# Sigmoid attention and two feed-forward layers on one core: first loads from two queues, values later, and products of zeros at the start

## Chip, cores and metric

The kernel runs on one core of a Trainium2 chip. The metric is the device time of one execution in microseconds (us). Three runs of the kernel before took 1111.2, 1111.86 and 1110.76 us; their median is 1111.2 us. A profiled execution is one more run, with its own time.

## What is computed

The inputs are float32 queries, keys and values of shape (4, 12, 448, 64), that is batch, heads, sequence and head size. The attention has a sigmoid in place of a softmax; two feed-forward layers over 1792 tokens follow. The reference, cut to what matters:

```python
scores = scale * np.matmul(q, k.transpose(0, 1, 3, 2)) - np.log(S)
attn = 1.0 / (1.0 + np.exp(-scores))
x = np.matmul(attn, v)                 # then (batch, S, heads * 64): 1792 x 768
h = x @ moe_w_in;  x = np.maximum(h, 0.0) ** 2 @ moe_w_out       # 768 -> 2048 -> 768
h = x @ moe2_w_in
out = (np.maximum(h, 0.0) + alpha * np.minimum(h, 0.0)) @ moe2_w_out
```

## The kernel before, in words

A unit is one batch entry and one pair of heads: 4 x 6 = 24 units, two heads of 64 rows side by side on the 128 partitions. Of the 448 positions of the sequence, 384 are three blocks of 128 (`MAIN`, `R = 3`) and 64 are a remainder (`REM`). Two units share their remainders, so the attention runs in 12 turns `d` of a loop over units `u = 2d` and `w = 2d + 1`. The order of all instructions is written out by hand: every engine takes its instructions in the order of the program (`tc.manual_schedule`), and each waits only for the data and buffers that it needs.

`fetch(d)` (lines 127 to 144) issues all loads of two units on SyncE's queue. Per unit these are two loads of queries, one for each head, into the tile `nat` (line 142), one of the queries' remainder into `qk` (line 144), three of the keys in the same way, one of the values (`v`, line 139) and one of their remainder (`vrem`, line 144): eight issues a unit, sixteen a turn. The tag `nat` has two buffers, so the next two units' queries can be issued only when the transposes of the last two are done.

`turn(u)` (lines 150 to 159) transposes queries and keys on TensorE (PE), seven transposes into a PSUM tile of the tag `big`, and VectorE copies the result to `flat`. `part(u)` and `rest(u)` (lines 161 to 167) split `flat` on VectorE into a rounded part and the difference. `scores(u, j)` (lines 169 to 178) makes the scores of one block of 128 keys with six products (three pairs; the second and third need the difference), and ScalarE takes the sigmoid out of PSUM. `last_scores(d)` (lines 180 to 188) does the same for the remainders of both units out of `flat`, eight products. The tag `big` has three buffers, shared in turn by transposes and scores. `values(u)` (lines 190 to 196) multiplies with the values, twelve products a unit, `last_values(d)` (lines 198 to 204) with the remainders, and `finish(u)` (lines 206 to 215) writes the result, split in two parts, into the x tiles on ScalarE and VectorE.

The start (lines 217 to 223) is `fetch(0)`, the load of alpha, `turn`, `part` and `rest` for units 0 and 1, then `fetch(1)`. A turn `d` of the loop (lines 224 to 257) has on PE, in this order: remainder scores of `d`, remainder values of `d - 1`, three score groups of `u`, values of `w - 2`, the transposes of units `u + 2` and `w + 2`, three score groups of `w`, values of `u`. In the first turn nothing of an earlier turn is there. SyncE's `fetch(d + 2)` stands behind the two transposes. Loads of the feed-forward weights (lines 66 to 72) and their assembly out of 64-bit floats are spread over later turns and the feed-forward layers. These (lines 268 to 361) run blocks of two 128-wide slices of the hidden layer over four tiles of tokens; their products are lines 276 and 309.

The program's first instructions are an identity matrix on GpSimd, a memset of the sigmoid's bias on VectorE, and a first sigmoid on one column, which brings ScalarE's function table (lines 113 to 116).

Of the kernel before, what the change touches and what calls it, by code (L numbers as in the profile page):

```python
# [9 lines left out]
F32 = mybir.dt.float32  # L10
# [5 lines left out]
P = 128  # L16
# [3 lines left out]
def fused_kernel(ctx: ExitStack, tc: tile.TileContext, q, k, v, w1i, w1o, w2i, w2o, alpha, out):  # L20
# [31 lines left out]
    wpool = ctx.enter_context(tc.tile_pool(name="wpool", bufs=1))  # L52

    eye = const.tile([P, P], F32, name="eye")
    bias = const.tile([P, 1], F32, name="bias")
    al = const.tile([P, NF], F32, name="al")


# [51 lines left out]
        return x[layer, t, c]  # L110

    with tc.manual_schedule():
        make_identity(nc, eye)
        nc.vector.memset(bias, -math.log(S))

        nc.scalar.activation(al[:, :1], bias, AF.Sigmoid)


        with tc.tile_pool(name="apool", bufs=1) as apool, tc.tile_pool(name="apsum", bufs=1, space=bass.MemoryType.PSUM) as psum:
            units = [(b, c) for b in range(B) for c in range(H // 2)]  # L120
            ND = len(units) // 2
            nats, qks, vals, vrems, flats, parts, sig, avs = {}, {}, {}, {}, {}, {}, {}, {}

            def half(u):
                return slice(u % 2 * REM, (u % 2 + 1) * REM)

            def fetch(d):
                if d >= ND:
                    return
                vrems[d] = apool.tile([P, 2, D], F32, tag="vrem", name=f"vrem{d}", bufs=3)  # L130
                for u in (2 * d, 2 * d + 1):
                    b, c = units[u]
                    hs = slice(2 * c, 2 * c + 2)
                    nats[u] = apool.tile([P, 2, R, 2, D], F32, tag="nat", name=f"nat{u}", bufs=2)
                    vals[u] = apool.tile([P, 2, R, D], F32, tag="v", name=f"v{u}", bufs=5)
                    qks[u] = apool.tile([P, 2, D], F32, tag="qk", name=f"qk{u}", bufs=2)
                    for j, src in enumerate((q, k, v)):
                        if j == 2:
                            nc.sync.dma_start(out=vals[u], in_=src[b, hs, :MAIN, :].rearrange("h (p r) d -> p h r d", r=R))
                        else:  # L140
                            for h in range(2):
                                nc.sync.dma_start(out=nats[u][:, j, :, h, :], in_=src[b, 2 * c + h, :MAIN, :].rearrange("(p r) d -> p r d", r=R))  # L142
                        last = (qks[u][:REM], qks[u][REM:], vrems[d][half(u)])[j]
                        nc.sync.dma_start(out=last, in_=src[b, hs, MAIN:, :].rearrange("h p d -> p h d"))

            def big(name):

                return psum.tile([P, 1024], F32, tag="big", name=name, bufs=3)

            def turn(u):  # L150

                ps = big(f"tp{u}")
                for r in range(R):
                    nc.tensor.transpose(ps[:, r * P:(r + 1) * P], nats[u][:, 0, r].rearrange("p h d -> p (h d)"), eye)  # L154
                nc.tensor.transpose(ps[:, MAIN:MAIN + P], qks.pop(u).rearrange("p h d -> p (h d)"), eye)
                for r in range(R):
                    nc.tensor.transpose(ps[:, 512 + r * P:512 + (r + 1) * P], nats[u][:, 1, r].rearrange("p h d -> p (h d)"), eye)  # L157
                flats[u] = apool.tile([P, 2 * S], F32, tag="flat", name=f"flat{u}", bufs=2)
                nc.vector.tensor_copy(flats[u], ps[:, :2 * S])

            def part(u):

                parts[u] = [apool.tile([P, 2 * S], F32R, tag=f"qk{p}", name=f"qk{p}{u}", bufs=3) for p in "hl"]
                nc.vector.tensor_copy(parts[u][0], flats[u])

            def rest(u):
                nc.vector.tensor_sub(parts[u][1], flats[u], parts[u][0])

            def scores(u, j):
                hi, lo = parts[u]  # L170
                ps = big(f"sc{u}_{j}").rearrange("p (h s) -> p h s", h=2)
                at = 512 + j * P
                for i, (kt, qt) in enumerate(((hi, hi), (hi, lo), (lo, hi))):
                    for h in range(2):
                        rows = slice(h * D, (h + 1) * D)
                        nc.tensor.matmul(ps[:, h, :S], kt[rows, at:at + P], qt[rows, :S], start=(i == 0), stop=(i == 2))  # L176
                sig[u, j] = apool.tile([P, 2, S], F32, tag="a", name=f"a{u}_{j}", bufs=5)
                nc.scalar.activation(sig[u, j], ps[:, :, :S], AF.Sigmoid, bias=bias, scale=SCALE)

            def last_scores(d):  # L180

                ps = big(f"scr{d}").rearrange("p (h s) -> p h s", h=2)
                for h in range(2):
                    rows = slice(h * D, (h + 1) * D)
                    for u in (2 * d, 2 * d + 1):
                        nc.tensor.matmul(ps[half(u), h, :S], flats[u][rows, S:S + REM], flats[u][rows, :S], start=True, stop=True)  # L186
                sig[d] = apool.tile([P, 2, S], F32, tag="ar", name=f"ar{d}", bufs=2)
                nc.scalar.activation(sig[d], ps[:, :, :S], AF.Sigmoid, bias=bias, scale=SCALE)

            def values(u):  # L190
                for j in range(R):
                    a = sig.pop((u, j))
                    if u % 2 == 0 and j == 0:
                        avs[u] = psum.tile([P, 512], F32, tag="av", name=f"av{u}", bufs=2)
                    for h in range(2):
                        nc.tensor.matmul(avs[u][h * D:(h + 1) * D, :S], vals[u][:, h, j, :], a[:, h, :], start=(u % 2 == 0 and j == 0), stop=(u % 2 == 1 and j == R - 1))  # L196

            def last_values(d):

                a, w, u = sig.pop(d), vrems.pop(d), 2 * d  # L200
                avs[u + 1] = psum.tile([P, 512], F32, tag="av", name=f"av{u + 1}", bufs=2)
                for h in range(2):
                    for i in (u, u + 1):
                        nc.tensor.matmul(avs[i][h * D:(h + 1) * D, :S], w[half(i), h, :], a[half(i), h, :], start=(i > u), stop=(i == u))  # L204

            def finish(u):
                b, c = units[u]
                ps = avs.pop(u)
                for t, (first, n) in enumerate(TILES):
                    lo, hi = max(first, b * S), min(first + n, (b + 1) * S)  # L210
                    if lo < hi:
                        xh, xl = (p[:, lo - first:hi - first] for p in x_tiles(0, t, c))
                        out_ = ps[:, lo - b * S:hi - b * S]
                        nc.scalar.activation(xh, out_, AF.Copy)
                        nc.vector.tensor_sub(xl, out_, xh)

            fetch(0)
            nc.sync.dma_start(out=al, in_=alpha.rearrange("(f p) -> p f", p=P))
            for u in (0, 1):
                turn(u)  # L220
                part(u)
                rest(u)
            fetch(1)
            for d in range(ND):
                u, w = 2 * d, 2 * d + 1

                i = d - 4
                last_scores(d)
                if d:
                    last_values(d - 1)  # L230
                    finish(u - 2)
                if 0 < i < 7:
                    assemble(i - 1, 1)
                for j in range(R):
                    scores(u, j)
                if d:
                    values(w - 2)
                if d + 1 < ND:
                    turn(u + 2)
                    turn(w + 2)  # L240
                    fetch(d + 2)
                if d:
                    finish(w - 2)
                if d + 1 < ND:
                    part(u + 2)
                    rest(u + 2)
                    part(w + 2)
                    rest(w + 2)
                if d in (1, 2, 3):
                    load(d - 1)  # L250
                if 0 <= i < 6:
                    assemble(i, 0)
                if 0 < i < 7:
                    split(i - 1)
                for j in range(R):
                    scores(w, j)
                values(u)
            last_values(ND - 1)
            finish(2 * ND - 2)
            values(2 * ND - 1)  # L260
            finish(2 * ND - 1)
# [130 lines left out]
```

## Time and profile before

| what | value |
|---|---|
| median of three runs | 1111.2 us (1110.76 to 1111.86) |
| the profiled execution's own time | 1112.57 us |
| its span, first to last instruction | 1110.8 us |
| mean granted clock of PE | 0.996 |
| busy: PE, VectorE, ScalarE, GpSimd | 1087.2, 691.8, 347.7, 154.5 us |

The span is one profiled execution. PE is the matrix engine, PEld its weight loads, DVE VectorE, ACT ScalarE, POOL GpSimd, SP SyncE, and SPq SyncE's queue of DMA issues. A row of the timeline gives start and length in us, engine, line, instruction, output and inputs with shapes, count, and in brackets how long the engine had been idle and what released it. Products are pipelined, so the length of one is more than the distance to the next. The granted clock (PEclk) is 1.00 at 2.4 GHz. A DMA share is the mean busy share of the core's 16 DMA engines.

### The profile page before, as it was taken

The numbers are of one execution on the slowest core, as the hardware profiler recorded it, in microseconds if no ns is written. First come the engines' busy times: TensorE is split into PE (matmuls) and PEld (weight loads), VectorE is DVE, ScalarE is ACT, GpSimd is POOL, SyncE is SP. The second block draws the span as 40 slices with busy tenths as digits, with TensorE's granted clock in tenths as the row PEclk, the third lists the DMA queues.
The fourth block names the chain that finished last, engine by engine and source line by source line (L and its number), as shares of the span: only waits on it lengthen the run. The fifth ranks groups of instructions, "written<-read, shape, count | busy, mean of one in ns | idle before, by whom it ended". The sixth has DMA issues, their size and how long they took to land.

```text
span 1110.8 us, 14450 instructions
## 1 busy us (share of the span) xinstructions
PE 1087.2 (98%) x5880; PEld 942.4 (85%) x5880; DVE 691.8 (62%) x991; ACT 347.7 (31%) x524; POOL 154.5 (14%) x94
## 2 busy tenths in 40 slices
PE   5999999999999999999999999999999999999998
PEld 3555557989898998989898999999999898989898
DVE  3458872345656575756666664577676767677554
ACT  2667773442222231323224444211121212021110
POOL 0001110020202020201014641101020201020000
PEclk9999999999999999999999999999999999999999
DMA  5575650020202121111111111202020202110015
GB/s 111 125 175 139 170 137 1 29 86 24 81 11 86 29 86 29 61 54 57 58 58 57 57 58 43 72 30 86 29 86 26 72 18 86 29 58 30 1 57 142
DMA packets 89266, 73.30 MB, mean 66 GB/s; under 512 B 52592, under 2 KB 83312, under 8 KB 89200
## 3 DMA queue, kind: packets, MB, share of 16 engines
q1 hardware_dynamic: 89200, 72.38, 22.8%
q8 instruction: 46, 0.75, 0.3%
q14 instruction: 20, 0.16, 0.0%
HBM read 66.85 MB, written 5.51 MB: 65 GB/s over the span
## 4 chain that ended last, share of the span: by engine, by line
PE 92%; DVE 4%; ACT 2%; SPq 1%; DMA 0%; issue 0%; ACTq 0%
PE h L276 40%; PE o L309 39%; PE av L196 5%; PE sc L176 5%; DVE raw L87 1%; SPq L142 1%; PE scr L186 1%; PE av L204 1%; DVE r L286 1%; PE tp L154 1%; DVE g L287 1%; PE tp L157 1%; ACT gh L288 1%; DVE raw L88 1%; ACT raw L83 1%; ACT wh L98 1%
## 5 line engine op out<-in xcount | busy, mean ns | idle before, releaser
L276 PE MATMUL h<-xh,wl 128*128 128x512 f32 (+1 forms) x768 | 278.5, 363 | 0.0
L276 PE MATMUL h<-xl,wh 128*128 128x512 f32 (+1 forms) x768 | 278.3, 362 | 0.0
L276 PE MATMUL h<-xh,wh 128*128 128x512 f32 (+1 forms) x768 | 277.9, 362 | 0.0
L314 DVE TENSOR_TENSOR acc<-o,acc 128x384 f32<-128x384 f32 (+1 forms) x364 | 200.1, 584 | 76.9 <-PE o L309 75.4
L99 POOL TENSOR_TENSOR wl<-raw,wh 128x768 fp32r<-128x768 f32 x64 | 124.2, 1941 | 883.8 <-ACT wh L98 835.8
L276 PEld LDWEIGHTS h<-xh,wh 128*128 128x128 f32 x768 | 144.2, 188 | 15.6 <-issue 0.7
L309 PE MATMUL o<-wh,gh 128*128 128x384 f32 x448 | 150.6, 336 | 6.5 <-DVE acc L314 6.2
L276 PEld LDWEIGHTS h<-xh,wl 128*128 128x128 f32 x768 | 144.1, 188 | 15.1
L276 PEld LDWEIGHTS h<-xl,wh 128*128 128x128 f32 x768 | 144.1, 188 | 15.0
L309 PE MATMUL o<-wl,gh 128*128 128x384 f32 x448 | 149.9, 335 | 0.0
L309 PE MATMUL o<-wh,gl 128*128 128x384 f32 x448 | 149.8, 334 | 0.0
L309 PE MATMUL o<-gh,wl 128*128 128x512 f32 (+1 forms) x384 | 139.1, 362 | 0.0
L309 PE MATMUL o<-gl,wh 128*128 128x512 f32 (+1 forms) x384 | 139.0, 362 | 0.0
L309 PE MATMUL o<-gh,wh 128*128 128x512 f32 (+1 forms) x384 | 138.9, 362 | 0.0
L288 ACT ACTIVATE gh<-g 128x512 fp32r<-128x512 f32 (+1 forms) x64 | 37.0, 579 | 284.6 <-DVE g L287 284.6
L289 DVE TENSOR_TENSOR gl<-g,gh 128x512 fp32r<-128x512 f32 (+1 forms) x128 | 93.5, 730 | 52.3 <-ACT gh L288 45.4
L98 ACT ACTIVATE wh<-raw 128x768 fp32r<-128x768 f32 x64 | 57.4, 897 | 175.3 <-DVE raw L88 129.4
L283 DVE SCALAR_TENSOR_TENSOR g<-h,r 128x512 f32<-128x512 f32 (+1 forms) x64 | 39.9, 623 | 113.4 <-ACT r L282 113.4
L87 DVE SCALAR_TENSOR_TENSOR raw<-raw 128x768 int32<-128x768 int32 x64 | 81.1, 1267 | 30.1 <-ACT raw L83 25.7
L282 ACT ACTIVATE r<-h 128x512 f32<-128x512 f32 (+1 forms) x64 | 34.8, 543 | 186.0 <-PE h L276 185.5
L309 PEld LDWEIGHTS o<-wh,gh 128*128 128x128 f32 x448 | 84.1, 188 | 9.4 <-DVE acc L314 8.1
L286 DVE TENSOR_SCALAR r<-h,al 128x512 f32<-128x512 f32 (+1 forms) x64 | 43.6, 681 | 71.4 <-PE h L276 71.3
(47 smaller groups left out, 1191.3 us busy)
## 6 DMA issues: line engine op xcount, KB each, us to landing
raw<-in_moe_w_in_dram SPq DMA_DIRECT2D x32, 768.0 KB, 4.9
raw<-in_moe_w_out_dram SPq DMA_DIRECT2D x32, 768.0 KB, 4.4
nat<-in_q_dram SPq DMA_DIRECT2D x48, 96.0 KB, 2.9
nat<-in_k_dram SPq DMA_DIRECT2D x48, 96.0 KB, 2.9
v<-in_v_dram SPq DMA_DIRECT2D x24, 192.0 KB, 2.9
out_dram<-acc SPq DMA_DIRECT2D x16, 192.0 KB, 2.7
out_dram<-acc SPq DMA_DIRECT2D x6, 384.0 KB, 2.3
qk<-in_q_dram SPq DMA_DIRECT2D x24, 32.0 KB, 2.6
```

Source lines behind the costliest of these rows:

```text
L87: nc.vector.scalar_tensor_tensor(out=low, in0=high, scalar=3, in1=low, op0=ALU.logical_shift_left, op1=ALU.bitwise_or)
L98: nc.scalar.activation(hi, w, AF.Copy)
L99: nc.gpsimd.tensor_sub(lo, w, hi)
L176: nc.tensor.matmul(ps[:, h, :S], kt[rows, at:at + P], qt[rows, :S], start=(i == 0), stop=(i == 2))
L196: nc.tensor.matmul(avs[u][h * D:(h + 1) * D, :S], vals[u][:, h, j, :], a[:, h, :], start=(u % 2 == 0 and j == 0), stop=(u % 2 == 1 and j = ...
L276: nc.tensor.matmul(ps[:, :n], wp[:, c * P:(c + 1) * P], xp, start=(c == 0 and i == 0), stop=(c == NC - 1 and i == 2))
L283: nc.vector.scalar_tensor_tensor(out=gt, in0=ps[:, :n], scalar=0.0, in1=r, op0=ALU.max, op1=ALU.mult)
L286: nc.vector.tensor_scalar(out=r, in0=ps[:, :n], scalar1=0.0, scalar2=al[:, f:f + 1], op0=ALU.min, op1=ALU.mult)
L288: nc.scalar.activation(gh, gt, AF.Copy)
L289: nc.vector.tensor_sub(gl, gt, gh)
L309: nc.tensor.matmul(ps[:, :size], *ops, start=(i == 0), stop=(i == len(turns) - 1))
L314: nc.vector.tensor_add(part, ps[:, :size], part)
```

## The change

The queries and keys of the first two turns (units 0 to 3) are issued at once at the start, queries on SyncE's queue and keys on ScalarE's. Units 2 and 3 get buffers of their own for this, borrowed from the weights' tag `woh`. Values are issued by a function of their own, `fetch_values`: behind the queries at the start, and later one turn ahead, behind the loads of queries and keys. The first sigmoid stands behind ScalarE's DMA issues and no longer writes into alpha's tile. `qk` has four buffers instead of two, `vrem` two instead of three. A tile of zeros is made first (in the storage of an x tile), and `keep_busy(n)` makes n products of zeros, 128 x 128 with 448 columns, which nothing reads: 10 before the first unit's transposes, 4 before the second unit's, 4 before the loop, and 6 in the first turn behind the remainder scores. The start's order is also changed: unit 1's transposes and their copy come before unit 0's difference.

```diff
--- before.py
+++ after.py
@@ -52,7 +52,7 @@
     wpool = ctx.enter_context(tc.tile_pool(name="wpool", bufs=1))
 
     eye = const.tile([P, P], F32, name="eye")
-    bias = const.tile([P, 1], F32, name="bias")
+    bias = const.tile([P, 2], F32, name="bias")
     al = const.tile([P, NF], F32, name="al")
 
 
@@ -110,10 +110,10 @@
         return x[layer, t, c]
 
     with tc.manual_schedule():
+        zeros = x_tiles(0, 0, 0)[0][:, :S]
+        nc.vector.memset(zeros.bitcast(F32), 0.0)
+        nc.vector.memset(bias, -math.log(S))
         make_identity(nc, eye)
-        nc.vector.memset(bias, -math.log(S))
-
-        nc.scalar.activation(al[:, :1], bias, AF.Sigmoid)
 
 
         with tc.tile_pool(name="apool", bufs=1) as apool, tc.tile_pool(name="apsum", bufs=1, space=bass.MemoryType.PSUM) as psum:
@@ -124,24 +124,32 @@
             def half(u):
                 return slice(u % 2 * REM, (u % 2 + 1) * REM)
 
-            def fetch(d):
+            def fetch(d, other=nc.sync):
+
                 if d >= ND:
                     return
-                vrems[d] = apool.tile([P, 2, D], F32, tag="vrem", name=f"vrem{d}", bufs=3)
                 for u in (2 * d, 2 * d + 1):
                     b, c = units[u]
                     hs = slice(2 * c, 2 * c + 2)
-                    nats[u] = apool.tile([P, 2, R, 2, D], F32, tag="nat", name=f"nat{u}", bufs=2)
+
+                    pool, tag, n = (wpool, "woh", 3) if d == 1 else (apool, "nat", 2)
+                    nats[u] = pool.tile([P, 2, R, 2, D], F32, tag=tag, name=f"nat{u}", bufs=n)
+                    qks[u] = apool.tile([P, 2, D], F32, tag="qk", name=f"qk{u}", bufs=4)
+                    for j, (src, queue) in enumerate(((q, nc.sync), (k, other))):
+                        for h in range(2):
+                            queue.dma_start(out=nats[u][:, j, :, h, :], in_=src[b, 2 * c + h, :MAIN, :].rearrange("(p r) d -> p r d", r=R))
+                        queue.dma_start(out=qks[u][j * REM:(j + 1) * REM], in_=src[b, hs, MAIN:, :].rearrange("h p d -> p h d"))
+
+            def fetch_values(d):
+                if d >= ND:
+                    return
+                vrems[d] = apool.tile([P, 2, D], F32, tag="vrem", name=f"vrem{d}", bufs=2)
+                for u in (2 * d, 2 * d + 1):
+                    b, c = units[u]
+                    hs = slice(2 * c, 2 * c + 2)
                     vals[u] = apool.tile([P, 2, R, D], F32, tag="v", name=f"v{u}", bufs=5)
-                    qks[u] = apool.tile([P, 2, D], F32, tag="qk", name=f"qk{u}", bufs=2)
-                    for j, src in enumerate((q, k, v)):
-                        if j == 2:
-                            nc.sync.dma_start(out=vals[u], in_=src[b, hs, :MAIN, :].rearrange("h (p r) d -> p h r d", r=R))
-                        else:
-                            for h in range(2):
-                                nc.sync.dma_start(out=nats[u][:, j, :, h, :], in_=src[b, 2 * c + h, :MAIN, :].rearrange("(p r) d -> p r d", r=R))
-                        last = (qks[u][:REM], qks[u][REM:], vrems[d][half(u)])[j]
-                        nc.sync.dma_start(out=last, in_=src[b, hs, MAIN:, :].rearrange("h p d -> p h d"))
+                    nc.sync.dma_start(out=vals[u], in_=v[b, hs, :MAIN, :].rearrange("h (p r) d -> p h r d", r=R))
+                    nc.sync.dma_start(out=vrems[d][half(u)], in_=v[b, hs, MAIN:, :].rearrange("h p d -> p h d"))
 
             def big(name):
 
...
-                nc.scalar.activation(sig[u, j], ps[:, :, :S], AF.Sigmoid, bias=bias, scale=SCALE)
+                nc.scalar.activation(sig[u, j], ps[:, :, :S], AF.Sigmoid, bias=bias[:, :1], scale=SCALE)
 
             def last_scores(d):
 
...
@@ -214,13 +222,28 @@
                         nc.scalar.activation(xh, out_, AF.Copy)
                         nc.vector.tensor_sub(xl, out_, xh)
 
-            fetch(0)
+            def keep_busy(n):
+
+                ps = psum.tile([P, 512], F32, tag="av", name=f"busy{n}", bufs=2)
+                for _ in range(n):
+                    nc.tensor.matmul(ps[:, :S], zeros[:, :P], zeros, start=True, stop=True)
+
+            fetch(0, nc.scalar)
+            fetch(1, nc.scalar)
+            fetch_values(0)
             nc.sync.dma_start(out=al, in_=alpha.rearrange("(f p) -> p f", p=P))
-            for u in (0, 1):
-                turn(u)
-                part(u)
-                rest(u)
-            fetch(1)
+
+            nc.scalar.activation(bias[:, 1:], bias[:, :1], AF.Sigmoid)
+            keep_busy(10)
+            turn(0)
+            part(0)
+            keep_busy(4)
+            turn(1)
+            rest(0)
+            part(1)
+            rest(1)
+            keep_busy(4)
+            fetch_values(1)
             for d in range(ND):
                 u, w = 2 * d, 2 * d + 1
 
@@ -229,6 +252,8 @@
                 if d:
                     last_values(d - 1)
                     finish(u - 2)
+                else:
+                    keep_busy(6)
                 if 0 < i < 7:
                     assemble(i - 1, 1)
                 for j in range(R):
@@ -239,6 +264,8 @@
                     turn(u + 2)
                     turn(w + 2)
                     fetch(d + 2)
+                    if d:
+                        fetch_values(d + 1)
                 if d:
                     finish(w - 2)
                 if d + 1 < ND:
```

## Rows read from the trace of the kernel before

**Rows 1.** The page's part 4: the chain that ended last, by engine

```profile
PE 92%; DVE 4%; ACT 2%; SPq 1%; DMA 0%; issue 0%; ACTq 0%
```

**Rows 2.** Waits of PE: engine line waited for: us in total, times, longest

```profile
PE tp L154 <- DMA nat<-in_q_dram: 8.0, 3, 4.6
PE o L309 <- DVE acc L314: 6.2, 6, 1.0
PE tp L155 <- DMA qk<-in_k_dram: 4.3, 3, 1.8
```

**Rows 3.** Windows: length, busy time of PE, PEld, DVE, ACT, POOL, PEclk, DMA share, GB/s

```profile
4.00:6.00 2.00, 0.87 (x3) 0.50 (x3) 0.00 (x0) 0.00 (x0) 0.00 (x0) 1.00 0.52 118
22.00:24.00 2.00, 0.52 (x3) 0.31 (x3) 0.00 (x0) 0.00 (x0) 0.00 (x0) 0.78 0.56 122
28.00:30.00 2.00, 2.00 (x12) 0.91 (x10) 1.94 (x3) 1.01 (x1) 0.00 (x0) 0.51 0.64 155
...
54.00:55.00 1.00, 1.00 (x10) 0.46 (x8) 0.97 (x3) 1.00 (x2) 0.00 (x0) 1.00 1.15 355
```

**Rows 4.** Timeline, PE, start and loop's second turn: start, length, line, tiles [idle before]

```profile
6.72 0.45 PE L155 MATMUL tp<-eye,qk 128*128 128x128 f32 x1 [1.28 <-DMA qk<-in_k_dram]
...
12.77 3.02 PE L186 MATMUL scr<-flat 64*64 64x448 f32 x8
...
19.37 0.70 PE L154 MATMUL tp<-eye,nat 128*128 128x128 f32 x3
...
24.43 0.45 PE L155 MATMUL tp<-eye,qk 128*128 128x128 f32 x1 [1.82 <-DMA qk<-in_k_dram]
...
31.91 0.98 PE L186 MATMUL scr<-flat 64*64 64x448 f32 x8
...
44.38 0.98 PE L186 MATMUL scr<-flat 64*64 64x448 f32 x8
```

**Rows 5.** Chain of waits in order of time, score products: start, length

```profile
25.52 3.66 PE sc L176 x18
...
33.65 2.02 PE sc L176 x18
```

**Rows 6.** Timeline, SyncE's DMA issues: start, length, line, tile

```profile
0.73 1.35 SPq L142 DMA_DIRECT2D nat<-in_q_dram  x2
...
4.12 0.62 SPq L144 DMA_DIRECT2D qk<-in_k_dram  x1
...
21.93 0.62 SPq L144 DMA_DIRECT2D qk<-in_k_dram  x1
...
39.02 1.23 SPq L142 DMA_DIRECT2D nat<-in_q_dram  x2
```

**Rows 7.** The page's part 6, one row: issues, KB each, us to landing

```profile
nat<-in_q_dram SPq DMA_DIRECT2D x48, 96.0 KB, 2.9
```

**Rows 8.** DMA view of 56.87 to 69.36 us, the same load

```profile
nat<-in_q_dram SPq DMA_DIRECT2D x4, 96.0 KB, 4.1
```

**Rows 9.** Timeline, VectorE and ScalarE at the start

```profile
0.73 1.28 ACT L116 ACT_TABLE_LOAD   x1 [0.73 <-PEq L376]
...
7.85 1.09 DVE L159 COPY flat<-tp 128x896 f32<-128x896 f32 x1 [6.99 <-PE tp L157]
...
8.97 0.63 DVE L164 CAST qkh<-flat 128x896 fp32r<-128x896 f32 x1
...
9.63 1.09 DVE L167 TENSOR_TENSOR qkl<-flat,qkh 128x896 fp32r<-128x896 f32 x1
...
15.84 1.01 ACT L188 ACTIVATE ar<-scr,bias 128x896 f32<-128x896 f32 x1 [13.61 <-PE scr L186]
```

**Rows 10.** Timeline, PE, the loop's second and third turn

```profile
35.60 2.48 PE L196 MATMUL av<-a,v 128*64 128x448 f32 x12
...
38.01 0.55 PE L154 MATMUL tp<-eye,nat 128*128 128x128 f32 x3
...
54.47 2.48 PE L196 MATMUL av<-a,v 128*64 128x448 f32 x12
```

More of the change, by code (lines that the diff above doesn't have):

```diff
@@ L187, in last_scores @@
                 sig[d] = apool.tile([P, 2, S], F32, tag="ar", name=f"ar{d}", bufs=2)
-                nc.scalar.activation(sig[d], ps[:, :, :S], AF.Sigmoid, bias=bias, scale=SCALE)
+                nc.scalar.activation(sig[d], ps[:, :, :S], AF.Sigmoid, bias=bias[:, :1], scale=SCALE)
             def values(u):
```

## The prediction

> **What bounds the kernel now.** I read the chain of waits first: TensorE (PE) carries 92% of it [rows 1]. So a change pays only where PE stands still or runs slowly, and the list of what PE waited for says where: 8.0 us in three waits for queries, 4.3 us in three waits for keys, and 6.2 us in the second layers for an accumulator [rows 2]. The waits for queries and keys all lie at the start, in the part that the diff rewrites. The windows show a second loss there: the granted clock is 1.00 at first, 0.78 on average in 22 to 24 us, 0.51 in 28 to 30 us, and 1.00 later [rows 3]. A granted 0.50 is the lower of PE's two levels, 1.2 against 2.4 GHz.
>
> The timeline shows more than the column. The transpose of the remainders takes 0.45 us at 24.43, at the low level, and the same 0.45 us at 6.72, under a granted 1.00 [rows 4]. So PE is at the low level from the start as well. Remainder scores begin at 12.77 and work is nearly unbroken from there; the transposes at 19.37 still take 0.70 us for three, where three at 38.01 take 0.55 [rows 4, 10], so I read the first rise as near 19.4, after 6.6 us. By the means of the windows the clock falls near 23.1 us, in a mostly idle stretch, and rises near 30.0, some 5.5 us after work resumed at 24.43 [rows 3, 4]. Two rises, then, after 5.5 and 6.6 us of work, mean 6.1. What a level is worth: 18 score products take 3.66 us of the chain at the low one and 2.02 at the high one [rows 5].
>
> From 31.91 us, where the loop's second turn begins with its remainder scores, PE is dense: the third turn begins at 44.38, so a turn is 12.47 us [rows 4]. What comes later hangs on PE's own pace, so **the gain is 31.91 us less the time at which the second turn begins afterwards**.
>
> **The change, part by part.** *Loads.* SyncE issues the first six loads of queries and keys from 0.73 to 4.74 us, one each 0.67 us; the keys' last, issued at 4.12, releases PE at 6.72: 2.6 us to land [rows 4, 6]. Unit 1's keys come at 11.74 because four value loads and six more stand in the queue, and unit 3's, issued at 21.93, only at 24.43, since SyncE waited for the transposes before fetching again [rows 4, 6]. Afterwards SyncE issues only queries of units 0 to 3 (12 issues, 0.73 to 8.7 us) and ScalarE the keys. No row has an issue by ScalarE. Below: 0.67 us each, side by side. Above: the two queues take turns and 24 issues need 16 us. I take the first, as SyncE's own issues are the nearest row, and keep the second as a rival. Then units 0, 1, 2 and 3 are wholly issued at 2.7, 4.7, 6.7 and 8.7 us.
>
> Do the transfers keep up? One queue keeps the DMA engines 0.52 busy at 118 GB/s [rows 3]; two ask for about 1.04 at 236 GB/s. The same engines show 355 GB/s at a share of 1.15 [rows 3], and where traffic is as dense a query load takes 4.1 us to land instead of 2.9 [rows 7, 8]. So I add 0.2 to 0.9 us to the landing: units land at about 5.5, 7.6, 9.6 and 11.6 us (uncontended: 4.8, 6.8, 8.8, 10.7). The Trainium skill, "DMA: Bandwidth & Descriptors", section "Rules for kernel authors", says that spreading transfers over issuing engines buys no bandwidth, only sequencer issue time. The rows agree that here issue time is what runs out; were the data path already full, the sum would be that of the second rival.
>
> *ScalarE.* Its table load (1.28 us [rows 9]) stood first; now it stands behind 12 issues: 8.7 + 1.3 + 0.2 = 10.2 us. Its cover is that the first remainder scores are not due before; if the issues are slower, the first sigmoid is what waits.
>
> *SyncE's other work.* Four value loads and alpha follow to 11.9 us, then the second four values to 14.5, then 12 loads of units 4 and 5 to 22.4, all landed by 25.0. They are due 6.1 us into the second turn (38.01 less 31.91), near 26.5 below: 1.5 us to spare [rows 4, 10]. In later turns queries and keys go first and values last, 12 + 4 issues (10.7 us) in a turn of 12.47.
>
> *Zero products.* The memset has no row; twice its columns are cast in 0.63 us [rows 9], so at most about 0.3 us, and PE can start near 1.4 us. Score products of 448 columns run as pairs, one on each half of the rows: 3.66 and 2.02 us for nine pairs are 0.41 and 0.22 us each [rows 5], gaps between groups included; for a zero product I take 0.38 at the low level and 0.20 at the high one. Ten cost 3.8 us, to 5.2, before unit 0 lands: free. They are work from 1.4 us on, so I put the rise at 1.4 + 6.1 = 7.5 us. The later 4, 4 and 6 are 14 × 0.2 = 2.8 us, mostly under the load and VectorE; below I charge what sticks out.
>
> *The first turn, step by step* (copy 1.09, cast 0.63, difference 1.09, sigmoid 1.01 [rows 9]; a unit's transposes 1.0 at the high level, from 38.01 to the next fetch at 39.02 [rows 6, 10], about 1.7 at the low one):
> Unit 0's transposes 5.5 to 7.2; copy to 8.35, cast to 9.0. Four zero products to 8.0, 0.4 past unit 1's landing. Unit 1's transposes to 9.0, copy to 10.1; unit 0's difference to 11.25, the rest of VectorE's chain to 13.0. Remainder scores 10.2 to 11.1, their sigmoid to 12.2. Six zero products 11.1 to 12.3, which is 1.0 us past unit 0's difference: that much is charged to the path. Three score groups of 0.6 us to 14.2; their sigmoids end at 14.0, 15.0 and 16.0. The big PSUM tag has three buffers, so unit 2's transposes go to 15.1, and unit 3's wait for the second sigmoid: 15.1 to 16.0. Their copies end at 16.25 and 17.3; unit 1's last score group waits for that second copy: to 18.0. Twelve value products, 2.4 us [rows 10], to 20.4.
> So the second turn begins at 20.4 instead of 31.91: **11.5 us less**. The profiled execution took 1112.57 us, which gives 1101.1; the median of the runs shown is 1.4 lower, 1111.2, and I forecast on it: **1099.7 us**. Bounds of this case: uncontended loads and a rise by 6 us begin the second turn at 19.0 or a little before (12.9 to 13.7 us less, 1097.5); fuller contention or a rise near 10 us, at 22.7 (1102).
>
> **The rivals.** *The clock rises late.* Zero data and transposes do not release it, only the scores do. Then both transposes, the zeros and the remainder scores run low: remainder scores 11.5 to 14.5, six zeros to 16.6, rise at 11.5 + 6.1 = 17.6, sigmoid-paced from there, unit 3's copy at 22.4, values to 25.5. That is 6.4 us less, 1104.8. For it: the sparse transposes before 12.77 brought no rise. Against it: ordinary products are ordinary work, and no row has products of zeros. The Trainium skill, "TensorE: Matmul & The Clock Gate", section "Part 4: PE-mode transpose", says that transposes do not count as busy for the clock; the trace agrees so far as it goes, but the zero products are no transposes.
>
> *The queues do not run side by side.* 24 issues at 0.67 us, shared: units issued at 4.7, 8.7, 12.8 and 16.8, unit 3 landing near 18.7; ScalarE's table is ready only at 18.0. Sigmoids then end at 19, 20, 21 and 22, unit 1's follow, values begin near 24 and the second turn at 26.4: 5.5 us less, 1105.7. For it: both queues use the same engines, and two ask for a share of 1.04. Against it: the 355 GB/s of [rows 3].
>
> *Slower.* Values are now fetched one turn later, behind 12 loads. After the transposes at 39.02, value loads would be issued from 46.9 and land by 49.8; the products that need them start at 54.47 [rows 6, 10], 4.6 us of slack. Only if values land later than that does PE wait in each turn; with ten turns, 1.15 us of wait in each eats the 11.5 us. At 6.6 us late each turn loses 2.0: 20 less 11.5 is 8.5 us slower, 1119.7. Against it: loads of these sizes land in 2.9 to 4.1 us even in dense traffic [rows 7, 8], and the weights' loads stand behind the values in SyncE's queue.
>
> **How the numbers follow.** Forecast 0.69; late clock 0.14, queues in turn 0.12, values late 0.03, something that gives the whole gain back 0.02. The range 1097.5 to 1105.0 holds the forecast's own bounds and the late clock; it leaves out the other three, 0.17. A measurement of this kernel tells about 0.2%, 2.2 us, from no change; all cases but the last two are faster by more: faster 0.95, same 0.02, slower 0.03.
>
> **What would show it.** The changed profile should show a ScalarE queue with keys from 0.73 us at a pitch near 0.67; zero products from about 1.4 us; 448-column products at a pitch of 0.20 us before 9 us; unit 3's transposes near 15 us without a wait for a load; ScalarE's table load near 8.7 us; remainder scores of the second turn near 20.4 us, and 12.47 us to the third. A second turn after 23 us, a turn that is longer, or a wait of PE for keys or values would make the forecast wrong; a ScalarE pitch of 1.3 us would name the second rival, score pairs at 0.41 us after 12 us the first.

## The result, and the profile after

The changed kernel takes 1101.18 us (median of five runs, 1101.0 to 1101.84) against 1111.2 us (1110.76 to 1112.52): 10.0 us less, a ratio of 0.9908 (95% interval 0.9893 to 0.9922). The profiled execution went from 1112.57 to 1101.18 us and its span from 1110.8 to 1099.4, 11.4 us less.

The chain and the waits of PE over the whole span, after; they answer to [rows 1] and [rows 2]:

```profile
PE 94%; DVE 4%; ACT 2%; issue 0%; ACTq 0%
```

```profile
PE o L336 <- DVE acc L341: 6.2, 6, 1.0
PE busy L229 <- DVE bias L115: 1.4, 1, 1.4
```

The waits for queries and keys are gone, 12.3 us of them before. What is left are the accumulator's 6.2 us, which the change doesn't touch, and 1.4 us at the very start, until VectorE has made the zeros. Here is the timeline of PE, with the columns of [rows 4] and [rows 10]:

```profile
5.33 0.87 PE L162 MATMUL tp<-eye,nat 128*128 128x128 f32 x3
...
7.80 0.49 PE L162 MATMUL tp<-eye,nat 128*128 128x128 f32 x3
...
9.46 1.42 PE L194 MATMUL scr<-flat 64*64 64x448 f32 x8
10.81 1.49 PE L229 MATMUL busy<-xh 128*128 128x448 f32 x6
12.23 0.47 PE L184 MATMUL sc<-qkh 64*128 64x448 f32 x2
...
20.62 0.98 PE L194 MATMUL scr<-flat 64*64 64x448 f32 x8
...
27.86 0.27 PE L163 MATMUL tp<-eye,qk 128*128 128x128 f32 x1
...
33.09 0.98 PE L194 MATMUL scr<-flat 64*64 64x448 f32 x8
```

The transposes at 5.33 and 7.80 us belong to units 0 and 1: three in 0.87 us, then three in 0.49. So the clock rose between them, and the third row, the remainder scores, runs at the high level. Unit 0's scores begin at 12.23 us. The second turn begins at 20.62 (31.91 before) and the third at 33.09: a turn is still 12.47 us, so the 11.3 us gained in the first turn are the whole gain. The windows (columns as in [rows 3]) and issues of the two queues, with ScalarE's first work among them:

```profile
4.00:6.00 2.00, 2.00 (x8) 1.47 (x8) 0.00 (x0) 0.00 (x0) 0.00 (x0) 1.00 0.99 222
14.00:16.00 2.00, 2.00 (x18) 1.49 (x14) 0.73 (x1) 1.95 (x3) 0.00 (x0) 1.00 0.76 44
22.00:24.00 2.00, 2.00 (x20) 1.61 (x18) 0.62 (x1) 1.85 (x3) 0.00 (x0) 1.00 0.50 112
```

```profile
0.74 1.30 ACTq L140 DMA_DIRECT2D nat<-in_k_dram  x2
...
9.35 0.63 ACTq L141 DMA_DIRECT2D qk<-in_k_dram  x1
...
9.65 0.62 SPq L141 DMA_DIRECT2D qk<-in_q_dram  x1
...
10.01 1.28 ACT L236 ACT_TABLE_LOAD   x1 [10.01 <-DMA qk<-in_k_dram]
...
11.41 0.99 ACT L196 ACTIVATE ar<-scr,bias 128x896 f32<-128x896 f32 x1
...
13.56 1.37 SPq L151 DMA_DIRECT2D v<-in_v_dram  x1
...
16.98 1.23 SPq L140 DMA_DIRECT2D nat<-in_q_dram  x2
...
24.71 0.62 SPq L141 DMA_DIRECT2D qk<-in_k_dram  x1
```

In 4 to 6 us the DMA engines are 0.99 busy at 222 GB/s, where one queue kept them 0.52 busy at 118 [rows 3]. The granted clock of 22 to 24 us is 1.00, not 0.78. ScalarE issues its twelve loads until 9.98 us and SyncE its until 10.27, so an issue takes 0.77 and 0.79 us on average, gaps included; the table load comes behind that, and the first sigmoid at 11.41 waits for it. In the experiments below, one execution of the kernel with one queue (e2) ran at a mean granted clock of 0.556 and took 1808.13 us; that kernel's median is of the other seven.

### The profile page after: what moved, and what is told of

It reads as the page before. It is cut to its first block, busy times and chain, and to the rows that moved or that the text cites. A ratio compares the mean times of both kernels' runs of the same rounds, so it can differ in the third digit from the quotient of the medians.

```text
span 1099.4 us, 14493 instructions
## 1 busy us (share of the span) xinstructions
PE 1086.7 (99%) x5904; PEld 944.6 (86%) x5904; DVE 691.6 (63%) x992; ACT 347.6 (32%) x524; POOL 154.6 (14%) x94
## 4 chain that ended last, share of the span: by engine, by line
PE 94%; DVE 4%; ACT 2%; issue 0%; ACTq 0%
PE h L303 40%; PE o L336 39%; PE av L204 5%; PE sc L184 5%; DVE raw L87 1%; PE scr L194 1%; PE tp L162 1%; PE av L212 1%; DVE r L313 1%; PE tp L165 1%; DVE g L314 1%; ACT gh L315 1%; PE busy L229 1%; DVE raw L88 1%; ACT raw L83 1%; ACT wh L98 1%
```

## The experiments

Each kernel was timed beside the kernel before, on the same chip; the last is the exception. The kernel before had medians of 1110.87 to 1111.51 us there, so a few tenths of a us between two experiments tell nothing. The figure to compare with is the changed kernel's 1101.18 us, second turn at 20.62, third at 33.09.

**No products of zeros (e1).**

```diff
             def keep_busy(n):
+                return
```

> The changed kernel without any product of zeros; all else as changed. Changed kernel: 1101.2 us, second turn of the loop at 20.6 us. Theory (the zero products raise the clock, the loads do the rest): PE starts at the low level with unit 0's transposes at 5.3 us; the low level lasts until near 11.5 or 16.5 us depending on whether the transposes count as work; transposes 1.7 us each, remainder scores end near 12.3, score groups 1.2 us each, so the second turn begins at 21.5 to 23 and the time is 1102 to 1104 us. Rival one (the zeros are only a cost on the path): the second turn comes 1 us earlier, 1100 us. Rival two (the zeros carry most of the gain): the clock is low for most of the first turn and falls again, second turn after 25 us, over 1105.5 us.

Measured: 1101.29 us, ratio 0.991 (0.9895 to 0.9926). That is the changed kernel's time: the 24 products add nothing to the gain that can be measured. The timeline of PE, and its one wait for a load in the second turn, say how that comes about:

```profile
7.26 0.90 PE L162 MATMUL tp<-eye,nat 128*128 128x128 f32 x3 [0.29 <-DMA nat<-in_q_dram]
...
8.95 2.52 PE L194 MATMUL scr<-flat 64*64 64x448 f32 x8
11.40 0.47 PE L184 MATMUL sc<-qkh 64*128 64x448 f32 x2
...
19.89 0.98 PE L194 MATMUL scr<-flat 64*64 64x448 f32 x8
```

```profile
PE tp L163 <- DMA qk<-in_k_dram: 0.5, 1, 0.5
```

Without zeros the transposes of unit 1 still run at the low level (0.90 us for three) and the remainder scores take 2.52 us instead of 1.42. But the clock is up by 11.40, 6.1 us after the first transposes (5.25), and there is no block of six zeros in the way, so unit 0's scores start 0.8 us earlier than in the changed kernel and the second turn at 19.89. Then units 4 and 5 are late: PE waits 0.5 us for unit 5's keys, and the third turn begins at 32.82, only 0.27 us before the changed kernel's. The theory's 1102 to 1104 us and the second rival's 1105.5 are wrong. The first rival has the second turn right and the time wrong: what the zeros cost on the path, the next wait takes back.

**One queue (e2).**

```diff
-            fetch(0, nc.scalar)
-            fetch(1, nc.scalar)
+            fetch(0)
+            fetch(1)
```

> The changed kernel with the keys of units 0 to 3 also on SyncE's queue. Theory (issue time is what runs out): 24 issues at 0.67 us, unit 0 landing near 6.9, unit 1 near 10.9, unit 2 near 15, unit 3 near 19 us; unit 3's transposes wait for the load until 19, its copy ends near 21, values to 24.2; second turn at 24 to 26 us, time 1104.7 to 1107 us, ScalarE's first sigmoid not late any more. Rival (the 16 DMA engines, not the issue, are full at the start, so one queue feeds them as well): unit 3 lands at 11.6 to 13 us as with two queues, and the time stays within 1 us of 1101.2.

Measured: 1108.51 us (1106.68 to 1109.76), ratio 0.9971 (0.9961 to 0.9982). The second queue is worth 7.3 of the 10.0 us. PE's timeline and windows:

```profile
23.69 0.98 PE L194 MATMUL scr<-flat 64*64 64x448 f32 x8
...
32.31 0.52 PE L162 MATMUL tp<-eye,nat 128*128 128x128 f32 x3 [1.21 <-DMA nat<-in_q_dram]
34.38 0.44 PE L163 MATMUL tp<-eye,qk 128*128 128x128 f32 x1 [1.55 <-DMA qk<-in_k_dram]
...
40.92 0.98 PE L194 MATMUL scr<-flat 64*64 64x448 f32 x8
```

```profile
4.00:6.00 2.00, 2.00 (x7) 1.44 (x6) 0.00 (x0) 0.00 (x0) 0.00 (x0) 1.00 0.51 115
...
34.00:36.00 2.00, 1.62 (x8) 1.27 (x10) 0.50 (x1) 0.00 (x0) 0.00 (x0) 0.60 0.51 115
```

The second turn begins at 23.69, near the theory's 24: 8.2 us earlier than in the kernel before, and 3.1 later than with two queues. The rest was missed by the theory: with 24 loads, the values and alpha ahead of it, the fetch of units 4 and 5 ends so late that PE waits 1.21 and 1.55 us in the second turn, the granted clock of 34 to 36 us is 0.60, and that turn takes 17.2 us. With one queue the DMA engines are at a share of 0.51 and 115 GB/s in 4 to 6 us, where two queues reach 0.99 and 222, so it is issue time that runs out there. The rival, that the engines would be full anyway, is excluded. The rule of the Trainium skill ("DMA: Bandwidth & Descriptors", section "Rules for kernel authors"), that a second issuing engine saves issue time alone, agrees with that: 115 GB/s became 222 because issuing was the limit.

**Zeros alone (e3).** The kernel before, with the 24 products of zeros and the changed order of unit 1's transposes; one queue, and the second pair fetched as before:

```diff
-            for u in (0, 1):
-                turn(u)
-                part(u)
-                rest(u)
+            keep_busy(10)
+            turn(0)
+            part(0)
+            keep_busy(4)
+            turn(1)
+            rest(0)
+            part(1)
+            rest(1)
+            keep_busy(4)
             fetch(1)
...
+                else:
+                    keep_busy(6)
```

> The kernel before with the 24 products of zeros at the places of the changed kernel, and unit 1's transposes before unit 0's difference; loads as before. Theory (the loads set the start, and the zeros pay only together with them): the clock is up by 8 us, the first scores run at the high level, but units 2 and 3 still land near 19 and 24.4 us, PE stands idle before them and the clock falls again; second turn at 30.5 to 32 us, time 1109.5 to 1111.5 us against 1111.2. Rival (the clock is most of what was lost): the clock stays high, unit 3's transposes and all behind them run at the high level, second turn near 28 us, 1107 us or less.

Measured: 1111.27 against 1111.51 us, ratio 1.0001 (0.9992 to 1.001): no difference. Its timeline and one window:

```profile
13.33 1.43 PE L188 MATMUL scr<-flat 64*64 64x448 f32 x8
...
21.56 0.52 PE L156 MATMUL tp<-eye,nat 128*128 128x128 f32 x3 [2.44 <-DMA nat<-in_q_dram]
23.56 0.30 PE L157 MATMUL tp<-eye,qk 128*128 128x128 f32 x1 [1.49 <-DMA qk<-in_k_dram]
...
30.08 0.98 PE L188 MATMUL scr<-flat 64*64 64x448 f32 x8
```

```profile
26.00:27.00 1.00, 1.00 (x8) 0.89 (x6) 1.00 (x2) 0.89 (x2) 0.00 (x0) 0.50 0.18 31
```

The remainder scores now run at the high level (1.43 us against 3.02). PE gets to unit 3's transposes sooner and waits there: 2.44 us, and 1.49 more for the keys. Then the clock falls, as it did before. The theory holds: a faster PE that has no data only waits longer. The second turn's 30.08 against 31.91 is no gain: this execution took 1110.59 us, 0.7 less than its kernel's median, and that of [rows 4] took 1112.57, 1.4 more than its own.

**Values fetched earlier (e4).** The values' large loads go back behind `fetch(d + 2)`, two turns ahead; `fetch_rests` issues the remainders, which stay one turn ahead:

```diff
-                    if d:
-                        fetch_values(d + 1)
+                    if d:
+                        fetch_rests(d + 1)
+                    fetch_values(d + 2)
```

> The changed kernel with the values' 384-row loads in the loop fetched two turns ahead, as the kernel before does (behind the queries and keys of that fetch); their remainders still one turn ahead. Theory (values one turn ahead have over 4 us to spare and cost nothing): second turn at 20.6, a turn 12.47 us, time within 0.4 us of 1101.2. Rival (values fetched late make PE wait somewhere in the loop): this one is faster by 1 us or more; or, the other way, SyncE's waits for a free value buffer come back and turns get longer, 1102 us or more.

Measured: 1101.48 us, ratio 0.9907 (0.9894 to 0.9921). The turns on PE:

```profile
20.98 0.98 PE L201 MATMUL scr<-flat 64*64 64x448 f32 x8
...
33.45 0.98 PE L201 MATMUL scr<-flat 64*64 64x448 f32 x8
```

A turn is 12.47 us, as with late values. Where the loop fetches its values has no effect that can be measured, in either direction.

**Transposes in place of zero products (e5).**

```diff
-                for _ in range(n):
-                    nc.tensor.matmul(ps[:, :S], zeros[:, :P], zeros, start=True, stop=True)
+                for _ in range(2 * n):
+                    nc.tensor.transpose(ps[:, :P], zeros.bitcast(F32)[:, :P], eye)
```

> The changed kernel with each product of zeros replaced by two transposes of zeros (128 columns), about the same length of work. Without zeros the clock rose near 11.2 us, 6 us after the first transposes at 5.25; with zeros near 7.3 us, 5.9 us after the first zero product at 1.38. Theory (transposes are work for the clock like any other): the clock rises near 7.5 us again, unit 1's transposes run three in 0.49 us, time within 0.5 us of 1101.2. Rival (transposes do not count): it rises only after the remainder scores, near 12 to 17 us; unit 1's transposes take 0.9 us for three and the second turn comes after 21.5 us, 1102.5 us or more.

Measured: 1101.6 us, ratio 0.9916 (0.9902 to 0.9929). PE's timeline:

```profile
1.48 4.50 PE L229 MATMUL busy<-eye,xh 128*128 128x128 f32 x20 [1.48 <-DVE bias L115]
5.77 0.84 PE L162 MATMUL tp<-eye,nat 128*128 128x128 f32 x3
...
6.62 0.52 PE L165 MATMUL tp<-eye,nat 128*128 128x128 f32 x3
```

Unit 0's last three transposes at 6.62 us take 0.52 us, the high level's length; the first three, at 5.77, took 0.84. So the clock rose after nothing but transposes since 1.48 us. Where the prediction weighed the rule of the Trainium skill ("TensorE: Matmul & The Clock Gate", section "Part 4: PE-mode transpose") that transposes don't count as busy, the measurement differs for the transposes of this kernel, and the measurement decides.

**Without the last six products (e7), and the same with an even number of PSUM tiles (e12).** e7 takes the six out; e12 also splits the four before the loop into two calls of two, which changes no product:

```diff
-                else:
-                    keep_busy(6)
...
-            keep_busy(4)
+            keep_busy(2)
+            keep_busy(2)
```

> The changed kernel without the six products of zeros behind the first turn's remainder scores; the other 18 stay. Theory (the gain is handed to the next wait): unit 0's scores start at 10.9 instead of 12.2, ScalarE's sigmoids, held by its table until 11.4, pace the rest, second turn near 19.9 instead of 20.6; but units 4 and 5 land near 27.6, so PE waits for their keys in the second turn and the third turn begins near 32.9 instead of 33.2: 1100.9 us, a gain of 0.3. Rival (the six are a plain 1.0 us on the path): third turn near 32.2, 1100.2 us or less. Second rival (without them the clock falls): 1102 us or more.

> The kernel of e7 (no last six) with the four products before the loop in two tiles of two. Theory (e7 lost 1.8 us to the buffer that its odd number of zero tiles shifted, and its own effect is the gain handed to the wait for units 4 and 5): no wait at the first feed-forward product, third turn 32.9 to 33.5, time 1100.6 to 1101.4 us. Rival (the six products are needed for the clock): 1102.5 us as e7.

Measured: e7 1102.68 us, ratio 0.9925 (0.9912 to 0.9937), slower than the changed kernel by 1.5; e12 1100.86 us, ratio 0.9905 (0.9891 to 0.992). e7 has a wait of PE that neither the changed kernel nor e12 has, and its timeline shows where:

```profile
PE h L301 <- DVE xl L223: 1.8, 1, 1.8
```

```profile
161.32 0.47 PE L301 MATMUL h<-xh,wh 128*128 128x512 f32 x1 [1.79 <-DVE xl L223]
```

It is at 161.32 us, at the first product of the feed-forward layers, which waits until the last attention output is taken out of PSUM. Every call of `keep_busy` takes the next of the two `av` buffers. With three calls instead of four, the attention's last output lies in the other one, and the layers' first tile is put on top of it. With four calls again (e12), or with none (e1), the wait is not there; e12 is 1.8 us faster than e7 with the same products. What remains of taking out the six is 0.3 us by the medians and nothing in the traces, as e12's PE and its wait for keys show:

```profile
5.24 0.49 PE L162 MATMUL tp<-eye,nat 128*128 128x128 f32 x3
...
19.71 0.98 PE L194 MATMUL scr<-flat 64*64 64x448 f32 x8
...
33.06 0.98 PE L194 MATMUL scr<-flat 64*64 64x448 f32 x8
```

```profile
PE tp L163 <- DMA qk<-in_k_dram: 0.9, 1, 0.9
```

The second turn begins 0.9 us earlier than in the changed kernel, and the third at 33.06, since PE waits 0.9 us for unit 5's keys. That is the theory of e7, with a wait of another place laid over it; in e7's own trace the two turns begin at 20.25 and 33.41, 0.3 and 0.5 us later than it said.

**The order of the queues (e9), without zeros (e10), and with an even number of tiles (e11).** ScalarE's table load goes between unit 1's and unit 2's keys, alpha and the second pair's values behind the fetch of units 4 and 5, and the six products are out:

```diff
             fetch(0, nc.scalar)
+            nc.scalar.activation(bias[:, 1:], bias[:, :1], AF.Sigmoid)
             fetch(1, nc.scalar)
...
-            nc.sync.dma_start(out=al, in_=alpha.rearrange("(f p) -> p f", p=P))
...
-            fetch_values(1)
...
-                    if d:
-                        fetch_values(d + 1)
+                    fetch_values(d + 1)
+                if d == 1:
+                    nc.sync.dma_start(out=al, in_=alpha.rearrange("(f p) -> p f", p=P))
```

e10 has the `return` of e1 as well, e11 the two calls of two.

> The changed kernel without the last six products of zeros, with ScalarE's first sigmoid (its table load) between unit 1's and unit 2's key loads, alpha's load moved behind the second turn's fetch, and the second pair's values behind the queries and keys of units 4 and 5. Theory (after the change the start is paced by ScalarE's table, then by SyncE's queue order): remainder sigmoid near 10.9, second turn near 19.4, units 4 and 5 landed by 24, no wait in the second turn, third turn near 31.9, time 1099.9 us. Rival (unit 3's keys, now 1.5 us later on ScalarE's queue, take the gain back; or the loads of 4 and 5 were not what the second turn would wait for): third turn at 32.8 or later, 1100.8 us or more.

> The kernel of e9 without any product of zeros. Theory (the zeros are worth what the later rise of the clock costs once nothing takes it back): rise near 11.2, remainder scores end near 11.4, second turn near 19.9, third near 32.4, 1100.4 us, 0.5 us more than e9. Rival (the zeros are worth nothing in any order): equal to e9 within 0.2 us.

> The kernel of e9 with the four products of zeros before the loop in two tiles of two, so that four PSUM tiles of zeros are made and not three; the 18 products are the same. e9 had a wait of 1.8 us at its first feed-forward product for the last attention output, which the changed kernel doesn't have. Theory (an odd number of zero tiles moves the last attention output into the PSUM buffer that the first feed-forward product takes over): the wait is gone, third turn near 32.6 as in e9, time 1100.7 us. Rival (the wait comes from the order of the queues): it stays, 1102.5 us.

Measured: e9 1102.56 us (0.9922, 0.991 to 0.9935), e10 1100.91 (0.9908, 0.9895 to 0.9922), e11 1100.49 (0.9902, 0.9887 to 0.9916). e9 has the odd number of tiles and its wait of 1.8 us; e11, without that wait, is 2.1 us faster. The wait for units 4 and 5 is gone, as expected. But the first sigmoid came no earlier, and its timeline says why:

```profile
6.28 0.20 ACT L232 ACTIVATE bias<-bias 128x1 f32<-128x1 f32 x1
...
10.99 0.66 ACTq L141 DMA_DIRECT2D qk<-in_k_dram  x1
...
11.70 1.01 ACT L196 ACTIVATE ar<-scr,bias 128x896 f32<-128x896 f32 x1 [5.22 <-DMA nat<-in_k_dram]
```

The table is loaded early, yet the sigmoid stands behind the keys of unit 3, which ScalarE issues until 11.65 us. So the rival of e9 was right about the start: unit 3's keys took most of the gain back. The second turn begins at 20.02 against a forecast of 19.4, and the third at 32.51, between the theory's 31.9 and the rival's 32.8. And e10 is within 0.4 us of e11, with the third turn at 32.74 and 32.76: as long as ScalarE's issues hold the first sigmoid, the zeros buy nothing that can be measured in this order either.

**Unit 3's keys on SyncE (e13).** As e11, with nine key loads on ScalarE instead of twelve (`last` is SyncE's queue unless it is given):

```diff
-                    for j, (src, queue) in enumerate(((q, nc.sync), (k, other))):
+                    for j, (src, queue) in enumerate(((q, nc.sync), (k, other if u % 2 == 0 else last))):
...
-            fetch(0, nc.scalar)
+            fetch(0, nc.scalar, nc.scalar)
```

> The kernel of e11 with unit 3's keys on SyncE's queue, so that ScalarE's queue has nine key loads and is free for the first sigmoid near 9.5 us. Theory (in e9 ScalarE issued its last key load until 11.65 and the remainder sigmoid waited for that): remainder sigmoid near 10.6 instead of 11.7, second turn near 19.3 instead of 20.0, third near 31.8, time 1099.8 us. Rival (unit 3's keys land late behind SyncE's queue and its transposes wait): second turn at 20 or later, 1100.7 us or more.

Measured: 1099.84 us (1099.52 to 1099.91), ratio 0.9894 (0.9878 to 0.9911). This is the fastest of all; its profiled span is 1098.1 against 1099.4 us. ScalarE's sigmoid and the turns:

```profile
10.94 1.01 ACT L196 ACTIVATE ar<-scr,bias 128x896 f32<-128x896 f32 x1 [3.71 <-DMA qk<-in_k_dram]
```

```profile
19.28 0.98 PE L194 MATMUL scr<-flat 64*64 64x448 f32 x8
...
31.77 0.98 PE L194 MATMUL scr<-flat 64*64 64x448 f32 x8
```

The first sigmoid is 0.5 us earlier than in the changed kernel, the second turn 1.3 and the third 1.3: what is gained at the start is kept, since units 4 and 5 are there in time and PE waits for no load.

**The kernel before once more (e14).**

> The kernel before once more, for its trace. Its times differ from run to run by 3 us (1109.1 to 1112.5), those of the changed kernel by less than 1. Theory (the clock at the start falls and rises at other times in each run): another second turn than 31.91 us, by as much as the span differs from 1110.8, with the low level ending at another time than 30.0 us; everything behind the second turn as before. Rival (the spread comes from the rest of the run): second turn at 31.9 again, and the difference lies behind it.

This execution had a granted clock of 0.81 in 18 to 20 us, 0.75 in 20 to 24, 0.50 in 26 to 28, and 0.75 from 30 us to its end, and took 1351.08 us. Its second turn began at 30.73, but under such a clock that says little on the question, which is taken up below under the median.

## Why the prediction was right, and where it was off

**The bound and the place of the gain: right.** The gain lies in the first turn alone, 31.91 to 20.62 us; later turns kept their 12.47.

**The loads: right in kind, short in size.** Side by side, both queues came close to the 0.67 us of one alone, but not to it: 0.77 and 0.79 us an issue, done at 9.98 and 10.27 us instead of 8.7. The share of 0.99 at 222 GB/s is near the sum's 1.04 at 236. It did no harm to units 0 to 3, whose transposes never waited. The same pitch shows that the rival of one shared issue path, 1.3 us an issue, is false, and e2 shows about what it would have cost: 7.3 us of the 10.0, more than the rival's sum, which stopped at the second turn's start. The later loads are another matter. The sum put the fetch of units 4 and 5 at 14.5 to 22.4 us with 1.5 us to spare. It ran from 16.98 to 25.33: SyncE's first loads were later, and the value load behind alpha took 1.37 us to issue instead of 0.60. The last load, issued at 24.71 and landing in some 2.5 us, is used at 27.86: about 0.6 us was left, and the two variants that began their second turn before 20 us without reordering SyncE's queue (e1, e12) gave their gain back there.

The prediction also misread why units 1 and 3 were late in the kernel before. Two value loads, not four, stand ahead of unit 1's keys. And SyncE's wait for transposes before unit 3's keys is short, as its waits in 11.9 to 15 us of that kernel show:

```profile
SPq L142 <- PE tp L157: 0.8, 1, 0.8
```

Before 24 us it has no other such wait. Thirty loads stand ahead of unit 3's last keys, and at 0.67 us each they alone put it at 20.8 us; it was issued at 21.93. So there too it was one queue's issue time.

**ScalarE: the cover was thinner than said.** The table was to be ready at 10.2 us; it was at 11.5, and the first sigmoid waited for it. The form of the sum was right, and the term 1.3 us too small; e13 takes it away.

**The zero products: the mechanism right, the worth wrong.** The rise was put at 7.5 us; it came between 6.7 and 7.8. That is partly luck: e12 starts with the same ten products at 1.39 us, and its clock was up by 5.24, where three transposes take 0.49 us. The charge of 1.0 us for the last six was near: unit 0's scores began at 12.23 against a forecast 12.3, and without the six the second turn begins 0.9 us earlier (e12). What was wrong is the price of a late rise. The forecast's own bound for a rise near 10 us had the second turn at 22.7 and 1102 us, and the rival of a late clock had 1104.8. In e1 the rise came near 11 us, an estimate from its remainder scores (2.52 us, where the eight take 3.02 at the low level [rows 4]); yet the second turn begins at 19.89, and the time is 1101.29. e1 is not quite that rival, which keeps the zeros on the path at the low level; but it and e5 show the assumption that failed, that only the scores release the clock. In e1 the clock had risen by 11.40 us, after transposes and remainder scores, and in e5 transposes were enough. So the zeros (e1, e3) and the later values (e4) are worth nothing that can be measured here. What is left for the 10 us is the loads, 7.3 of them by the second queue (e2). The changed order of unit 1's transposes was not tried by itself; together with the zeros it gained nothing (e3).

**The first turn: right.** The second turn was forecast at 20.4 and begins at 20.62; from unit 0's scores (12.23 against 12.3) to the value products (18.22 against 18.0) the sum is within about 0.2 us. Remainder scores 0.7 us earlier (9.46 against 10.2) and a first sigmoid 0.3 us later (11.41 against 11.1) did not show in it, since the six zero products held PE until 12.23 anyway.

**The median: the step that failed.** The sum gave 11.5 us on the profiled execution, 1101.07 us, and the profiled execution measured 1101.18. The forecast of 1099.7 took the same 11.5 off the median of 1111.2. The profiled execution of the kernel before had been 1.4 us above its median, and the changed kernel's is not: its times lie within 0.84 us of each other. So 11.5 us was what one long execution had to lose, and the median had 10.0.

The times of the kernel before go with the mean granted clock of the execution. Of 35 executions, those of the comparisons and the profiled one, three at 1.000 took 1109.07 to 1109.20 us, sixteen at 0.997 or 0.998 took 1110.63 to 1111.56, and sixteen at 0.996, the profiled one among them, took 1111.69 to 1112.57. All five of the changed kernel have 0.999 or 1.000. In the profiled execution every window below 1.00 lies between 22 and 30 us. Where the lower clock lies in the others is not shown, so that it is the start that makes the spread stays argued.

**Slower, by late values: excluded.** e4 moved them and the time stayed.

## What to carry to other kernels

When one queue's issue time (0.67 us a load here) is what the first work waits for, spread the first loads over a second queue and go on to look at what is behind them in both queues: the same engine's first computation, and the next fetch, are now late. A stall that is shortened shows its worth only if the next wait is not already there, so take out one part at a time and read where the gain goes. And when a filler takes a rotating buffer, count its turns: one call more or less moved a 1.8 us wait to the other end of the attention.

## What had not been expected of the hardware

Transposes of zeros bring the clock up as zero products do (e5). The load of alpha, 8 KB, keeps the DMA engines busy while next to nothing moves: in 14 to 16 us of the changed kernel their share is 0.76 at 44 GB/s, and the issue behind it takes 1.37 us; in e2, where alpha is issued at 19.25, the share is 0.73 at 53 GB/s in 20 to 22 us, and the issue behind it takes 2.92 us. And the two queues that issue together in the changed kernel stop for 0.8 to 0.9 us after their first five loads (ScalarE between 4.04 and 4.83 us, SyncE between 4.33 and 5.21), which the one queue of e2 doesn't do in its 24 loads. Why is not shown.
